# Fused pooled attention and Fourier-mixing feed-forward on one core: blocks mixed into attention in longer stretches, full price for a change of kind, one product per mean

## Chip, cores and metric

One Trainium2 chip, one core. The metric is the device time of one launch in microseconds, the median of several runs of the same program.

## What is computed

```python
q_pool = q.reshape(B, H, S // 2, 2, D).mean(axis=3)        # B 4, H 8, S 1152, D 64
attn = softmax(scale * q_pool @ k.T)                       # 576 x 1152 per head
x = (attn @ v), heads side by side                         # (4, 576, 512)
mixed = real(fft(fft(x, axis=1), axis=2))
u = x + mixed
un = (u - mean(u)) / sqrt(var(u) + 1e-6)                   # over the 512 features
out = u + relu(un @ w_ch1) @ w_ch2                         # 512 -> 2048 -> 512
```

Everything is float32. Products that need the accuracy are done as three products of high and low parts.

## The kernel before

The kernel is written by a planner that runs while the program is built: class `Model` keeps a clock for each engine, and `loop` chooses, piece by piece, what TensorE does next. The instructions then stand in that order in the program, on every engine.

**Attention.** 16 head pairs (four per batch), each with five units of 128 query columns. A unit on TensorE is three kinds of work. `S` (`s_piece`): score products of keys and queries, three pieces of 384 keys, high and low parts (`ksh`, `ksl`, `qh`, `ql`); VectorE scales each piece out of PSUM and takes the row extreme. `T` (`t_step`): transposes of the exponentials `sp` (ScalarE makes them in `s_exp`); VectorE or ScalarE copies them to `pt` and `ptc`. `AV` (`av`): products of `vs` and `pt` into the one bank `o`. The scores and transposes use 64 rows of the array, AV uses 64 columns, all else the full array.

**The middle of a batch** (`mid`, that is `dft` then `norm`): when four pairs are done, the two Fourier transforms are products with constant matrices (tiles `cc`, `cs`, `xs`, `bs`, `y`), then the mean over features (`lsum` with the matrix `onesm` of 1/512: two products per half of the columns, accumulated), the subtraction, the squares (`sq` with `onesm`), one over the root (`vt`, `dg`), and the high and low parts `unh`, `unl`. Its steps for VectorE, ScalarE and GpSimd are generators that `poll` drains whenever the engine would be free.

**The feed-forward** (`ffn`): per batch 32 blocks of 12 products, alternating four blocks with `w1` on `unh`, `unl` and four with `w2` on `g`. Batches 0 to 2 have blocks of 512 tokens; the last batch takes its own 576 and the 64 left over from each of the others in 64 blocks of 384 tokens. From the moment batch 0's middle is through, blocks are mixed into attention as filler: `spend` adds TensorE time to a `credit`, `block` takes it off, and the loop lets a block in while the credit is above 0 and its operands are ready (`fit`), or when nothing else is ready for `WAIT` of planner time. Behind the last pair `background` runs what is left; when no block fits it calls `force`, which takes the next step of the first waiting list, the middle of the batch ahead of the others.

**What sets the order.** For each candidate the loop adds, to the planner's time at which it is ready, `TURN` and half the entry of `SWITCH` if the kind of work changes:

```python
c = {k: max(t, now) + BIAS[k] + (0 if nc.mode == MODE[k] else TURN + 0.5 * SWITCH.get((nc.mode, MODE[k]), 130)) ...}
if fills and not lag[0]:
    if credit > 0 and fit():
```

**The start.** `load_first` brings the first pair in parts: keys in three parts, queries in the column ranges `Q0`; a part is pooled (two columns added), rounded to `qh` on ScalarE and subtracted to `ql`, on VectorE for the first part and on GpSimd for the others. Unit 0 needs columns 0 to 128, unit 1 columns 128 to 256.

Line 191 is the planner's call into the real instruction, so all rows have that line; rows are told apart by the tiles.

Of the kernel before, what the change touches and what calls it, by code (L numbers as in the profile page):

```python
# [195 lines left out]
class Pool:  # L196
# [4 lines left out]
    def tile(self, shape, dt, tag=None, name=None, bufs=None, **kw):  # L201
# [8 lines left out]
        if len(ring) == (bufs or self.bufs):  # L210
# [7 lines left out]
SWITCH = {("S", "T"): 95, ("T", "S"): 10, ("T", "AV"): 160, ("F", "S"): 222, ("T", "F"): 216, ("F", "AV"): 224, ("S", "AV"): 225,  # L218
          ("S", "F"): 285, ("S", "T1"): 95, ("T1", "S"): 10}
# [95 lines left out]
def fused_kernel(ctx: ExitStack, tc: tile.TileContext, k2, q2, v2, w1, w2, cst, out):  # L315
# [89 lines left out]
    Q0 = [(0, 128), (128, 512), (512, QW)]  # L405
# [112 lines left out]
    def den_recip(pr):  # L518
# [24 lines left out]
        if pr % 4 == 3:  # L543
            mids.append(Stream(mid(pr // 4), FIRST))
            started.append(pr // 4)

    def attention():
        idle = gp.tile([P, 512], F32, tag="g", name="zero")
        nc.vector.memset(idle, 0.0)
        ps = bank()  # L550
        for n in (512, 512, 192):
            nc.tensor.matmul(ps[:, :n], lhsT=idle[:, :P], rhs=idle[:, :n], start=True, stop=True)
        q_load, q_part, k_load, k_part, v_load = load_first()
        k_load(*K0[0])
        q_load(*Q0[0])
        for c in K0[1:]:
            k_load(*c)
        nc.sync.dma_start(ident, cst[4, :, :P])
        q_load(*Q0[1])
        v_load()  # L560
        q_load(*Q0[2])
        units = [(pr, j) for pr in range(NP) for j in range(5)]
        k_part(*K0[0])
        q_part(*Q0[0])
        k_part(*K0[1])
        k_part(*K0[2])
        for pc in range(3):
            s_piece(0, 0, pc)
        q_part(*Q0[1])
        s_exp(0, 0)  # L570
        s_exp(1, 0)
        nc.sync.dma_start(onesm, cst[4, :, P:2 * P])
        q_part(*Q0[2])
        loop(units)

    def loop(units):
# [136 lines left out]
        while at["a"][0] < n:  # L713
# [8 lines left out]
            c = {k: max(t, now) + BIAS[k] + (0 if nc.mode == MODE[k] else TURN + 0.5 * SWITCH.get((nc.mode, MODE[k]), 130)) for k, t in c.items() if t is not None}  # L722
            if fills and not lag[0]:
                if credit > 0 and fit():
# [14 lines left out]
    TURN = 100  # L739
    EXPS = 50  # L740
# [107 lines left out]
    def norm(b):  # L848
# [8 lines left out]
        for t in range(2):  # L857
            c = slice(t * HT, t * HT + HT)
            got = []

            def mean():
                got.append(bank())
                for j in range(2):
                    nc.tensor.matmul(got[0][:, :HT], lhsT=onesm, rhs=sm[:, j, c], start=j == 0, stop=j == 1)

            yield "pe", [sm[:, 0, c], sm[:, 1, c]], mean
# [257 lines left out]
    class Stream:  # L1124

        def __init__(self, gen, limit=None):
            self.gen, self.step, self.since, self.limit = gen, None, 0.0, limit or LIMIT
# [13 lines left out]
    def advance(s, pe=False, force=False):  # L1141
# [10 lines left out]
        if c[0] == "pe":  # L1152
            if not force and (not pe or nc.ready(*c[1]) > now + 50 or nc.slot("ps_t", "t", 7, 1) > now + 100):
                return False
# [46 lines left out]
    def spend(pe, at=False):  # L1201
        nonlocal credit
        credit = min(credit + pe * RATES[nb], 4000.0)
# [28 lines left out]
    WAIT, FLOOR = 500, -6000  # L1232

    def force():
        for s in list(mids)[:1] + streams:
            c = advance(s, True, True)
            if c:
                return True
            if c is None:
                if s in mids:  # L1240
                    mids.remove(s)
                else:
                    streams.remove(s)
                return True
        return False

    def background():

        while mids or fills or (tail[0] and streams):
            poll(True)  # L1250
            if fills and credit > 0 and fit():
                block()
                continue
            if not tail[0]:
                return
            if fills and fit():
                block()
            elif not force():
                if not (fills and block()):
                    return  # L1260
# [81 lines left out]
```

## Time and profile before

| | |
|---|---|
| median of 3 runs | 924.02 us (923.2 to 924.3) |
| profiled execution, its own time | 923.16 us |
| its span, first to last instruction | 921.4 us |
| TensorE busy | 895.4 us (97%) |
| VectorE busy | 592.0 us (64%) |
| ScalarE busy | 457.0 us (50%) |
| GpSimd busy | 289.6 us (31%) |
| mean granted TensorE clock | 0.996 |
| chain that ended last | TensorE 78%, VectorE 9%, ScalarE 5% |

TensorE's busy time includes ends that are modelled, so a wait of a few hundred nanoseconds between two products of the pipeline hides in it; for such waits the starts of successive rows are compared. The program has four stretches: attention alone (to about 235 us), attention with feed-forward blocks in between (to about 664 us), the middle of the last batch among blocks of batch 2 (to about 732 us), and feed-forward alone. A pair of rows with the same tiles is one instruction's two halves only for products of plain float32 (the mean, the squares, AV); a product of rounded float32 has one record.

### The profile page before, as it was taken

The numbers are of one execution on the slowest core, as the hardware profiler recorded it, in microseconds if no ns is written. First come the engines' busy times: TensorE is split into PE (matmuls) and PEld (weight loads), VectorE is DVE, ScalarE is ACT, GpSimd is POOL, SyncE is SP. The second block draws the span as 40 slices with busy tenths as digits, with TensorE's granted clock in tenths as the row PEclk, the third lists the DMA queues.
The fourth block names the chain that finished last, engine by engine and source line by source line (L and its number), as shares of the span: only waits on it lengthen the run. The fifth ranks groups of instructions, "written<-read, shape, count | busy, mean of one in ns | idle before, by whom it ended". The sixth has DMA issues, their size and how long they took to land.

```text
span 921.4 us, 22672 instructions
## 1 busy us (share of the span) xinstructions
PE 895.4 (97%) x9046; PEld 754.9 (82%) x9046; DVE 592.0 (64%) x1621; ACT 457.0 (50%) x916; POOL 289.6 (31%) x379
## 2 busy tenths in 40 slices
PE   8999998999999999999999999999999999999998
PEld 6888887787877788778777778887877788999998
DVE  6898889888769787779578655455474523222222
ACT  5678887769576468666444363545420311110110
POOL 4335456585438464555231330300030000000000
PEclk9999999999999999999999999999999999999999
DMA  6453664154675665777752242523284456543432
GB/s 217 132 177 106 217 207 133 61 189 156 215 263 219 202 238 205 259 237 282 250 197 70 104 136 91 186 70 105 80 249 134 129 189 211 192 135 117 135 92 69
DMA packets 54413, 153.27 MB, mean 166 GB/s; under 512 B 15186, under 2 KB 18018, under 8 KB 54308
## 3 DMA queue, kind: packets, MB, share of 16 engines
q1 hardware_dynamic: 49972, 142.20, 46.9%
q0 software_dynamic: 2160, 8.85, 2.9%
q8 instruction: 71, 1.16, 0.5%
q10 hardware_dynamic: 2176, 0.79, 0.3%
q14 instruction: 34, 0.28, 0.1%
HBM read 129.06 MB, written 22.75 MB: 165 GB/s over the span
## 4 chain that ended last, share of the span: by engine, by line
PE 78%; DVE 9%; ACT 5%; issue 4%; POOL 2%; DMA 1%; SPq 0%; DVEq 0%; ACTq 0%; POOLq 0%
PE f L191 46%; PE o L191 13%; PE s L191 12%; PE t L191 7%; DVE sp L191 3%; DVE pt L191 2%; ACT sp L191 2%; ACT pt L191 1%; POOL xs L191 1%; DVE wa L191 1%; DVE x L191 1%; DVE xs L191 1%; DMA qr<-in_q 1%; DVE d L191 0%; POOL wa L191 0%
## 5 line engine op out<-in xcount | busy, mean ns | idle before, releaser
L191 PE MATMUL f<-g,w 128*128 128x512 f32 (+1 forms) x960 | 211.6, 375 | 0.2 <-DVE sp L191 0.2
L191 ACT ACTIVATE sp<-sp,bia 128x1152 f32<-128x1152 f32 x144 | 180.2, 1257 | 38.4 <-DVE sp L191 37.9
L191 PEld LDWEIGHTS f<-g,w 128*128 128x128 f32 x960 | 173.7, 189 | 26.7 <-issue 2.8
L191 PE MATMUL f<-unh,w 128*128 128x512 f32 (+1 forms) x640 | 188.5, 376 | 0.0
L191 DVE TENSOR_SCALAR_CACHE_REDUCE sp<-s,bia 128x384 f32<-128x384 f32 x288 | 162.9, 612 | 15.5 <-PE s L191 12.3
L191 ACT ACTIVATE g<-f 128x512 fp32r<-128x512 f32 (+1 forms) x80 | 44.4, 555 | 234.5 <-PE f L191 234.5
L191 PE MATMUL o<-pt,vs 128*64 128x128 f32 (+1 forms) x2560 | 149.1, 266 | 2.4 <-ACT x L191 1.7
L191 PEld LDWEIGHTS o<-pt,vs 128*64 128x64 f32 x2560 | 127.1, 137 | 25.6 <-issue 19.1
L191 PEld LDWEIGHTS f<-unh,w 128*128 128x128 f32 x640 | 116.0, 188 | 18.5 <-issue 2.9
L191 DVE COPY pt<-t 128x512 f32<-128x512 f32 x143 | 92.3, 683 | 54.0 <-PE t L191 53.7
L191 PE MATMUL s<-ksh,qh 64*128 64x384 f32 (+1 forms) x432 | 111.2, 394 | 9.7 <-DVE pt L191 3.2
L191 PE MATMUL f<-unl,w 128*128 128x512 f32 (+1 forms) x320 | 118.0, 369 | 0.0
L191 DVE TENSOR_TENSOR x<-f,x 128x512 f32<-128x512 f32 (+1 forms) x80 | 47.7, 597 | 107.2 <-PE f L191 107.1
L191 DVE SCALAR_TENSOR_TENSOR g<-f,g 128x512 fp32r<-128x512 f32 (+1 forms) x80 | 50.8, 635 | 100.4 <-ACT g L191 100.3
L191 PEld LDWEIGHTS t<-ident,sp 64*128 64x128 f32 x2592 | 93.1, 139 | 24.9 <-issue 15.7
L191 PE MATMUL t<-ident,sp 64*128 64x64 f32 x2592 | 106.2, 226 | 2.9 <-DVE sp L191 1.3
L191 ACT COPY pt<-t 128x512 f32<-128x512 f32 x145 | 79.0, 590 | 36.9 <-PE t L191 36.0
L191 PE MATMUL s<-ksh,ql 64*128 64x384 f32 (+1 forms) x432 | 95.2, 348 | 0.6 <-POOL ql L191 0.6
L191 PE MATMUL s<-ksl,qh 64*128 64x384 f32 (+1 forms) x432 | 91.3, 338 | 0.0
L191 DVE TENSOR_SCALAR_CACHE_REDUCE sp<-s 128x384 f32<-128x384 f32 x144 | 74.7, 551 | 17.3 <-PE s L191 16.3
L191 POOL TENSOR_TENSOR wa<-wa,wk 128x256 int32<-128x256 int32 x64 | 47.3, 759 | 114.2 <-DVE wa L191 79.5
L191 PEld LDWEIGHTS s<-ksh,qh 64*128 64x128 f32 (+1 forms) x432 | 55.6, 188 | 33.6 <-DVE pt L191 8.2
(97 smaller groups left out, 1024.4 us busy)
## 6 DMA issues: line engine op xcount, KB each, us to landing
w<-w SPq DMA_DIRECT2D x128, 512.0 KB, 3.7
wraw<-in_w SPq DMA_DIRECT2D x32, 512.0 KB, 4.3
w<-wraw SPq DMA_DIRECT2D x32, 512.0 KB, 3.3
qr<-in_q SPq DMA_DIRECT2D x15, 640.0 KB, 4.8
vs<-in_v SPq DMA_DIRECT2D x16, 576.0 KB, 3.8
ksh<-in_k POOLq DMA_DIRECT2D x15, 576.0 KB, 6.0
kr<-in_k SPq DMA_DIRECT2D x15, 576.0 KB, 7.1
out<-x SPq DMA_DIRECT2D x12, 256.0 KB, 3.7
```

What stands on the lines that cost most here:

```text
L191: return real(*args, **kw)
```

## The change

- **Full price.** A change of kind is charged with the whole entry of `SWITCH` instead of half; the entries for transposes to scores go from 10 to 70 and for transposes to AV from 160 to 150.
- **Stretches by credit.** A block is let in by credit only above a threshold that depends on what TensorE is doing: 0 behind AV, 1000 behind scores or transposes, and down to -2000 behind another block. The credit may grow to 8000 instead of 4000, and `WAIT` goes from 500 to 300.
- **One product per mean.** The two halves of `lsum` are added by VectorE or GpSimd first, and the mean is one product instead of two, twice per batch.
- **Smaller first query loads.** The second query part is columns 128 to 256 instead of 128 to 512, the rest follows in two parts, and the load of the second part is issued ahead of the constant `ident`.
- **The end by readiness.** `background` lets a block in whenever one fits, and otherwise `force` takes whatever is ready first by the planner's clock: the next block, the middle of the batch or another list, instead of the first list in a fixed order.
- A parameter `SOFT` is added with the value 0, which changes nothing.

```diff
--- before.py
+++ after.py
@@ -215,8 +215,8 @@
         return t
 
 
-SWITCH = {("S", "T"): 95, ("T", "S"): 10, ("T", "AV"): 160, ("F", "S"): 222, ("T", "F"): 216, ("F", "AV"): 224, ("S", "AV"): 225,
-          ("S", "F"): 285, ("S", "T1"): 95, ("T1", "S"): 10}
+SWITCH = {("S", "T"): 95, ("T", "S"): 70, ("T", "AV"): 150, ("F", "S"): 222, ("T", "F"): 216, ("F", "AV"): 224, ("S", "AV"): 225,
+          ("S", "F"): 285, ("S", "T1"): 95, ("T1", "S"): 70}
 
 
 def _pe(m, op, out, ins, kw):
@@ -402,7 +402,7 @@
             mybir.DependencyClass.Sync, mybir.DependencyReason.DATA), reason="later than the first heads")
 
     K0 = [(i * 384, i * 384 + 384) for i in range(3)]
-    Q0 = [(0, 128), (128, 512), (512, QW)]
+    Q0 = [(0, 128), (128, 256), (256, 512), (512, QW)]
 
     def load_first():
 
@@ -541,7 +541,7 @@
         for c in (slice(0, HT), slice(HT, SQ)):
             yield ("pool", "dve") if pr % 4 < 3 else ("dve", "pool"), lambda e: ENG[e].tensor_tensor(x[:, c], x[:, c], big[:, c], op=ALU.mult)
         if pr % 4 == 3:
-            mids.append(Stream(mid(pr // 4), FIRST))
+            mids.append(Stream(mid(pr // 4), FIRST, SOFT if 0 < pr // 4 < B - 1 else 0))
             started.append(pr // 4)
 
     def attention():
@@ -555,10 +555,11 @@
         q_load(*Q0[0])
         for c in K0[1:]:
             k_load(*c)
+        q_load(*Q0[1])
         nc.sync.dma_start(ident, cst[4, :, :P])
-        q_load(*Q0[1])
         v_load()
         q_load(*Q0[2])
+        q_load(*Q0[3])
         units = [(pr, j) for pr in range(NP) for j in range(5)]
         k_part(*K0[0])
         q_part(*Q0[0])
@@ -571,6 +572,7 @@
         s_exp(1, 0)
         nc.sync.dma_start(onesm, cst[4, :, P:2 * P])
         q_part(*Q0[2])
+        q_part(*Q0[3])
         loop(units)
 
     def loop(units):
@@ -719,9 +721,9 @@
             exp()
             now = nc.t["pe"]
             c = {k: f() for k, f in (("s", s_cand), ("t", t_cand), ("a", a_cand))}
-            c = {k: max(t, now) + BIAS[k] + (0 if nc.mode == MODE[k] else TURN + 0.5 * SWITCH.get((nc.mode, MODE[k]), 130)) for k, t in c.items() if t is not None}
+            c = {k: max(t, now) + BIAS[k] + (0 if nc.mode == MODE[k] else TURN + SWITCH.get((nc.mode, MODE[k]), 130)) for k, t in c.items() if t is not None}
             if fills and not lag[0]:
-                if credit > 0 and fit():
+                if credit > THR.get(nc.mode, 0) and fit():
                     block()
                     continue
                 if (not c or min(c.values()) > now + WAIT) and credit > FLOOR and fit():
@@ -737,6 +739,8 @@
     BIAS = {"s": 0.0, "t": 0.0, "a": 0.0}
     MODE = {"s": "S", "t": "T", "a": "AV"}
     TURN = 100
+    THR = {"AV": 0, "S": 1000, "T": 1000, "F": -2000, "M": 0}
+    SOFT = 0
     EXPS = 50
 
     def room(pr, j):
@@ -856,14 +860,16 @@
         vt = smp.tile([HT // 3, 6], F32, tag="vt", name="vt")
         for t in range(2):
             c = slice(t * HT, t * HT + HT)
+            yield SB, lambda e: ENG[e].tensor_tensor(sm[:, 0, c], sm[:, 0, c], sm[:, 1, c], op=ALU.add)
+        for t in range(2):
+            c = slice(t * HT, t * HT + HT)
             got = []
 
             def mean():
                 got.append(bank())
-                for j in range(2):
-                    nc.tensor.matmul(got[0][:, :HT], lhsT=onesm, rhs=sm[:, j, c], start=j == 0, stop=j == 1)
-
-            yield "pe", [sm[:, 0, c], sm[:, 1, c]], mean
+                nc.tensor.matmul(got[0][:, :HT], lhsT=onesm, rhs=sm[:, 0, c], start=True, stop=True)
+
+            yield "pe", [sm[:, 0, c]], mean
             ps = got[0]
             d = mtile([P, 4, HT], F32, "d")
             for i, u in enumerate((ua, ub)):
@@ -1123,8 +1129,8 @@
 
     class Stream:
 
-        def __init__(self, gen, limit=None):
-            self.gen, self.step, self.since, self.limit = gen, None, 0.0, limit or LIMIT
+        def __init__(self, gen, limit=None, soft=0):
+            self.gen, self.step, self.since, self.limit, self.soft = gen, None, 0.0, limit or LIMIT, soft
 
         def peek(self):
             if self.step is None:
@@ -1150,7 +1156,7 @@
             return False
         now = nc.t["pe"]
         if c[0] == "pe":
-            if not force and (not pe or nc.ready(*c[1]) > now + 50 or nc.slot("ps_t", "t", 7, 1) > now + 100):
+            if not force and (not pe or nc.mode in MODE.values() and now - s.since < s.soft or nc.ready(*c[1]) > now + 50 or nc.slot("ps_t", "t", 7, 1) > now + 100):
                 return False
             c[2]()
         else:
@@ -1200,7 +1206,7 @@
 
     def spend(pe, at=False):
         nonlocal credit
-        credit = min(credit + pe * RATES[nb], 4000.0)
+        credit = min(credit + pe * RATES[nb], 8000.0)
         poll(at)
 
     def step(queue):
@@ -1229,35 +1235,42 @@
             step(fills)
         return need[0] is not None and nc.ready(*need[0]) <= nc.t["pe"] + 100 and nc.slot("ps_t", "t", 7, 1) <= nc.t["pe"] + 100
 
-    WAIT, FLOOR = 500, -6000
+    WAIT, FLOOR = 300, -6000
+
+    def when(s):
+
+        c = s.peek()
+        if c is False:
+            return 0.0, s
+        if c is None:
+            s.step = None
+            return 1e12, s
+        if c[0] == "pe":
+            return max(nc.ready(*c[1]), nc.slot("ps_t", "t", 7, 1)), s
+        return min(nc.probe(c[1], e) for e in c[0] if e != "now"), s
 
     def force():
-        for s in list(mids)[:1] + streams:
-            c = advance(s, True, True)
-            if c:
-                return True
-            if c is None:
-                if s in mids:
-                    mids.remove(s)
-                else:
-                    streams.remove(s)
-                return True
-        return False
+        best = min((when(s) for s in list(mids)[:1] + streams), key=lambda x: x[0], default=(1e12, None))
+        if need[0] is None and fills:
+            step(fills)
+        if need[0] is not None and max(nc.ready(*need[0]), nc.slot("ps_t", "t", 7, 1)) <= best[0]:
+            return block()
+        s = best[1]
+        if best[0] >= 1e12:
+            return bool(fills) and block()
+        if advance(s, True, True) is None:
+            if s in mids:
+                mids.remove(s)
+            else:
+                streams.remove(s)
+        return True
 
     def background():
 
-        while mids or fills or (tail[0] and streams):
+        while mids or fills or streams:
             poll(True)
-            if fills and credit > 0 and fit():
-                block()
-                continue
-            if not tail[0]:
+            if not (fills and fit() and block()) and not force():
                 return
-            if fills and fit():
-                block()
-            elif not force():
-                if not (fills and block()):
-                    return
 
     def conversions():
         nonlocal cdue
```


Three places in the two programs' orders show how instructions move. In them `o` is AV, `t` a transpose, `s` a score product, `f<-g` or `f<-unh`, `f<-unl` a feed-forward block, `f<-lsum`, `f<-onesm,sq` and `f<-dg` the middle of a batch.

TensorE near the end of attention (pair 15), before: one block stands inside a unit's AV products.

```order
L191 MATMUL s<-ksl,qh 128x384 x2
L191 MATMUL o<-pt,vs 64x128 x6
L191 MATMUL f<-g,w_9092 128x512 x12
L191 MATMUL o<-pt,vs 64x128 x10
L191 MATMUL o<-ptc,vs 64x128 x2
L191 MATMUL t<-ident,sp 128x64 x36
```

The same unit of the changed program:

```order
L191 MATMUL s<-ksl,qh 128x384 x2
L191 MATMUL f<-g,w_9784 128x512 x12
L191 MATMUL f<-g,w_9918 128x512 x12
L191 MATMUL o<-pt,vs 64x128 x16
L191 MATMUL o<-ptc,vs 64x128 x2
L191 MATMUL t<-ident,sp 128x64 x36
```

Two blocks now stand ahead of AV, and the AV products of a unit are not parted. Over the whole of attention 60 blocks in 59 separate places become 58 blocks in 43 places, and the number of times that the kind of work changes on TensorE (scores, transposes, AV, blocks, the middle, the transposes of `den`) goes from 435 to 414; counted by the part of the array that is in use (64 rows, 64 columns, all) it goes from 296 to 287.

TensorE in the last batch's middle, from the second mean to the spread of one over the root, before:

```order
L191 MATMUL f<-lsum,onesm 128x288 x2
L191 MATMUL f<-unh,w_10943 128x512 x2
L191 MATMUL f<-unl,w_10943 128x512
...
L191 MATMUL f<-unl,w_10943 128x512
L191 MATMUL f<-onesm,sq 96x1 x6
L191 MATMUL f<-g,w_10963 128x512 x12
L191 MATMUL f<-dg,onesm 128x288
L191 MATMUL f<-g,w_10987 128x512 x12
L191 MATMUL f<-dg,onesm 128x288
```

Changed:

```order
L191 MATMUL f<-lsum,onesm 128x288
L191 MATMUL f<-unh,w_10947 128x512 x2
L191 MATMUL f<-unl,w_10947 128x512
...
L191 MATMUL f<-unl,w_10947 128x512
L191 MATMUL f<-g,w_10967 128x512 x12
L191 MATMUL f<-g,w_10991 128x512 x12
L191 MATMUL f<-onesm,sq 96x1 x6
L191 MATMUL f<-g,w_11016 128x512 x12
L191 MATMUL f<-g,w_11047 128x512 x12
L191 MATMUL f<-dg,onesm 128x288
```

The mean is one product, three blocks instead of one stand between the second mean and the squares, and two blocks instead of one stand behind them. Ahead of this, nine blocks instead of seven stand between the last AV product and the first Fourier product (`f<-cs,xs`).

GpSimd at the start, before:

```order
L191 TENSOR_TENSOR ksl<-kr,ksh 128x192 x4
L191 TENSOR_TENSOR qr<-qr 128x384
L191 TENSOR_TENSOR ql<-qr,qh 128x384
L191 TENSOR_TENSOR qr<-qr 128x128
L191 TENSOR_TENSOR ql<-qr,qh 128x128
L191 DMA ksh<-in_k 128x1152
```

Changed:

```order
L191 TENSOR_TENSOR ksl<-kr,ksh 128x192 x4
L191 TENSOR_TENSOR qr<-qr 128x128
L191 TENSOR_TENSOR ql<-qr,qh 128x128
L191 TENSOR_TENSOR qr<-qr 128x256
L191 TENSOR_TENSOR ql<-qr,qh 128x256
L191 TENSOR_TENSOR qr<-qr 128x128
L191 TENSOR_TENSOR ql<-qr,qh 128x128
```

GpSimd does the 128 columns that unit 1 needs first, then 256 columns instead of having them in the same instruction. On SyncE the load of these 128 columns stands ahead of `ident` instead of behind it, and the load of the other 256 columns behind the load of `vs`. ScalarE rounds the 256 columns behind the first two exponentials, where it rounded the last 128 before.

## Rows read from the trace of the kernel before

**Rows 1.** The page, busy time and share of the span by engine.
```profile
PE 895.4 (97%) x9046; PEld 754.9 (82%) x9046; DVE 592.0 (64%) x1621; ACT 457.0 (50%) x916; POOL 289.6 (31%) x379
```

**Rows 2.** Busy us (x instructions) by stretch: PE, PEld, DVE, ACT, POOL; then PEclk, DMA.
```profile
43.00:235.00 192.00, 183.42 (x2822) 156.93 (x2818) 166.54 (x520) 156.57 (x314) 109.72 (x143) 1.00 0.47 155
120.00:165.00 45.00, 41.15 (x673) 35.04 (x669) 41.94 (x129) 37.67 (x73) 30.98 (x41) 1.00 0.45 147
235.00:664.00 429.00, 423.31 (x4444) 339.19 (x4442) 294.78 (x784) 237.36 (x485) 152.06 (x197) 1.00 0.53 180
728.00:732.00 4.00, 4.00 (x12) 3.07 (x12) 0.89 (x3) 2.22 (x8) 0.00 (x0) 0.61 0.34 86
```

**Rows 3.** TensorE waits, 43 to 235 us: total, times, longest; first and last of 10.
```profile
PE s L191 <- DVE pt L191: 2.4, 5, 1.2
...
PE t L191 <- ACT sp L191: 0.2, 1, 0.2
```

**Rows 4.** The same from 235 to 664 us; first and last of 10.
```profile
PE f L191 <- ACT y L191: 1.3, 1, 1.3
...
PE s L191 <- DVE sp L191: 0.2, 1, 0.2
```

**Rows 5.** Order of time at the start: start, length, engine, line, operation, [idle <-releaser].
```profile
8.69 0.99 POOL L191 TENSOR_TENSOR qr<-qr 128x384 f32<-128x384 f32 x1 [0.78 <-DMA qr<-in_q]
...
10.28 0.44 PE L191 MATMUL s<-ksh,qh 64*128 64x384 f32 x2 [1.87 <-ACT qh L191]
...
11.36 0.69 PE L191 MATMUL s<-ksh,ql 64*128 64x384 f32 x2 [0.64 <-POOL ql L191]
...
11.38 1.24 ACT L191 ACTIVATE sp<-sp,bia 128x1152 f32<-128x1152 f32 x1
...
14.08 1.38 PE L191 MATMUL t<-ident,sp 64*128 64x64 f32 x36
```

**Rows 6.** Order of time on TensorE, the mean products of batch 0.
```profile
192.33 2.21 PE L191 MATMUL f<-lsum,onesm 128*128 128x288 f32 x8
...
194.47 0.44 PE L191 MATMUL s<-ksh,qh 64*128 64x384 f32 x2
```

**Rows 7.** Order of time on TensorE, where the kind of work changes.
```profile
657.15 1.97 PE L191 MATMUL o<-pt,vs 128*64 128x128 f32 x32
658.94 0.39 PE L191 MATMUL o<-ptc,vs 128*64 128x128 f32 x4
659.26 0.77 PE L191 MATMUL t<-ident,sp 64*128 64x64 f32 x18
659.97 0.73 PE L191 MATMUL f<-unh,w 128*128 128x512 f32 x2
...
662.82 0.27 PE L191 MATMUL t<-ident,den 128*9 128x128 f32 x1
```

**Rows 8.** Order of time on TensorE, feed-forward blocks one behind the other.
```profile
740.28 0.62 PE L191 MATMUL f<-unh,w 128*128 128x512 f32 x2
...
743.00 0.62 PE L191 MATMUL f<-unh,w 128*128 128x512 f32 x2
```

**Rows 9.** Order of time on TensorE, from transposes to score products.
```profile
95.09 0.42 PE L191 MATMUL s<-ksh,qh 64*128 64x384 f32 x2
95.35 0.34 PE L191 MATMUL s<-ksh,ql 64*128 64x384 f32 x2
95.53 0.33 PE L191 MATMUL s<-ksl,qh 64*128 64x384 f32 x2
```

**Rows 10.** Order of time on TensorE, the last batch behind attention.
```profile
685.83 0.43 PE L191 MATMUL f<-cs,xs 128*97 128x128 f32 x2 [1.28 <-DVE xs L191]
...
724.10 0.67 PE L191 MATMUL f<-onesm,sq 128*96 128x1 f32 x6 [0.70 <-POOL sq L191]
...
726.18 0.64 PE L191 MATMUL f<-onesm,sq 128*96 128x1 f32 x6 [1.42 <-DVE sq L191]
726.68 4.58 PE L191 MATMUL f<-g,w 128*128 128x512 f32 x12
731.08 0.67 PE L191 MATMUL f<-dg,onesm 96*128 96x288 f32 x2
```


## The prediction

> **What bounds the kernel.** I read the share of busy time by engine first: TensorE 97% of the span, VectorE 64%, ScalarE 50% [rows 1]. That alone says that work taken off TensorE counts nearly in full, but also that the page's idle time (26 us) is an upper bound on what better hiding can show there. The stretches come second [rows 2]. From 43 to 235 us, attention with nothing to fill in, TensorE is idle for 192.0 - 183.4 = 8.6 us and VectorE is busy for 166.5 of 192 us, 87%; from 120 to 165 us it is 41.9 of 45, 93%, and there TensorE is idle for 3.85 us. From 235 to 664 us, with blocks to fill in, TensorE is idle for 5.7 us of 429. So TensorE is the bound, with VectorE close behind in the first stretch only. The list of waits is third: in both stretches they are many and short, at most 1.2 to 1.3 us for one, down to 0.2 [rows 3, 4]. Last, in order of time, the two ends, where whole gaps stand [rows 5, 10], and the places where the kind of work changes [rows 7 to 9].
>
> **The change, part by part.**
>
> *One product per mean.* Eight products of batch 0's and its like's means go (two per batch, four batches). In batch 0 four of them, eight records, take 192.33 to 194.47 = 2.14 us up to the next score product [rows 6]. Of that some 0.15 us is the change of kind, so a record is 0.25 us and a product 0.5; eight are **-3.9 us**. With nothing taken off it would be 4.3, and if half were covered 2.0. Eight additions of 288 columns come in, on VectorE or GpSimd; TensorE stands among blocks or score products there, so I cost them at nothing. In the last batch, where the chain is bare, they are counted under the end.
>
> *Fewer changes of kind.* 435 become 414, 21 fewer. What one costs: four AV records take 658.94 to 659.26 = 0.32 us, where the 32 ahead of them take 1.79, 0.056 each; so leaving AV costs 0.32 - 0.22 = 0.10. A block behind transposes takes 659.97 to 662.82 = 2.85 us [rows 7], one behind another block 740.28 to 743.00 = 2.72 [rows 8]; so entering a block costs 0.13. A change is thus 0.1 if one side pays, 0.23 if both do; I take 0.15, since most changes that go are those around a block, which pay on both sides, but leave a cheaper one behind. 21 x 0.15 = **-3.2 us**, between -2.1 and -4.8. The credit thresholds do this: the blocks move from 59 places to 43.
>
> From transposes to scores, both on 64 rows of the array, the first score pair takes 95.09 to 95.35 = 0.26 us and the next 0.18 [rows 9], so 0.08 is paid without any change of the array's division; the new entry of 70 in the table is near that, the old 10 was not. The Trainium skill (TensorEngine Tiling (Array Packing), Key Properties) says that a change of the tiling mode drains TensorE, and that using another tile of the same mode does not. By that rule alone only the 296 to 287 mode changes would count, 9 x 0.15 = 1.4 us, and the whole sum would be 1.8 us smaller. The trace agrees as to the modes, but shows a price inside one as well, so I keep 3.2.
>
> *The end.* Three gaps of the last batch's middle stand open [rows 10]: 1.28 us ahead of the first Fourier product, which waits for VectorE's `xs`; 0.70 and 1.42 us ahead of the two groups of squares. Behind them TensorE runs the next block, 12 products, from 726.68 to 731.08 = 4.40 us instead of 2.72: the clock granted from 728 to 732 us is 0.61 of full speed on average [rows 2], and it fell behind the gaps. That is 1.28 + 2.12 + 1.68 = 5.1 us. The new order has two blocks more ahead of the Fourier product (5.4 us against 1.3 missing) and two more ahead of the squares (5.4 against 2.1). The extra addition before the mean (0.44 to 0.86 us by the neighbours' lengths on VectorE and GpSimd) fits in that cover as well. I take **-5.0 us**; the ends are 0 (the blocks then wait for their weights instead) and -5.1. With no gap there, nothing should lower the clock.
>
> *The start.* The products of unit 1 wait 1.87 us for `qh` and 0.64 us for `ql` [rows 5]: GpSimd gets the 384 columns at 8.69 us and needs 0.99 us for the first of two like steps. With 128 columns first, loaded earlier, GpSimd can begin when it is free (0.78 us before 8.69), the first step is about a third as long, and the scores of unit 1 can begin near 8.7 instead of 10.28. What is late next is the second exponential, which ends at 11.38 + 1.24 and does not move, because it hangs on VectorE's work on unit 0; the transposes, at 14.08 now, can then start for the first head at once and be done some 2 us sooner. The other 256 columns are rounded behind the exponentials and may hold unit 2 for a few tenths. **-1.8 us**, between 0 and -2.5 (both waits). SyncE issues one more load; `ident`, which moves behind it, is needed only for those transposes, more than 8 us later.
>
> *The rest of attention.* Every unit is reordered, so the short waits fall elsewhere. Nothing in the trace prices the new ones. The bounds: all visible idle from 43 to 664 us goes, -14.3, or there is as much again, +14.3. I take **0**, since the same work meets the same engines and the mean wait is a few tenths of a microsecond.
>
> Sum: -3.9 - 3.2 - 5.0 - 1.8 = -13.9 us. The profiled execution took 923.16 us (span 921.4, 1.8 around it), so 909.3; the median of the runs is 0.9 above that execution, so **910.0 us**.
>
> **Rivals.**
>
> *Waits left open (slower).* Filling in fewer places takes the cover away from 16 spots where a block stood. If each then shows a wait as long as the longest of today, 1.2 us [rows 3], that is +19.2 against -13.9: 929. It turns from gain to loss at 13.9 / 16 = 0.87 us a spot. For it: the thresholds of 1000 behind scores and transposes keep blocks out exactly where the waits for VectorE and ScalarE are. Against: most waits are 0.2 to 0.5 us, and a wait over `WAIT`, now 300, still lets a block in.
>
> *VectorE takes over.* In the first stretch it has 7 to 13% left [rows 2]. The first blocks come later (none by the end of the eighth pair, where there were five), so that stretch grows by about 14 us of TensorE work without cover. If the rate of 120 to 165 us, 3.85 us idle in 45, held for 45 us more, that is +3.9, and the start's 1.8 would be given back: 915.7. The Trainium skill (the same page, PSUM Bottleneck) warns of this: packing small products speeds TensorE up, but not the copies out of PSUM, which can become the bound. The trace bears it out for one stretch of 45 us, not for the whole.
>
> *The end waits for weights.* If the blocks moved forward there find their weights late, the 5.0 us turn into another wait: 915.0. For it: seven blocks in a row each need a tile of weights. Against: blocks in a row run at 2.72 us from 740 us on [rows 8].
>
> *Waits shrink too.* If the truer prices halve the visible idle between 43 and 664 us (14.3), it is 7 us better: 903.
>
> *The change does nothing* is excluded by the order of the programs.
>
> **How the numbers follow.** The forecast, with some microseconds either way for the reordered waits: 0.45. VectorE: 0.20. Weights late: 0.10. Waits shrink: 0.13. Several of the losses together, ending near 924: 0.05. Waits left open: 0.07. A measurement of this kernel can tell 0.2%, 1.85 us, from no change. So faster 0.88, no difference 0.05, slower 0.07. The range holds the first four cases with their spread, 903 to 919 us, and leaves out the last two and the edges of the others, about 2 in 10.
>
> **What would show it.** Right: 16 records of the mean instead of 32; no wait of a microsecond ahead of `f<-cs,xs` and the squares of the last batch, and the granted clock at 1.00 throughout that part; the scores of unit 1 near 8.7 us; the last block's start some 13 us earlier. The prediction is wrong if TensorE's idle time from 43 to 664 us is up by several microseconds, if the waits for VectorE grow above all in the first stretch, or if blocks in the last part wait for loads.

## The result and the profile after

| | before | after |
|---|---|---|
| median, four runs each in turn | 923.61 us (922.11 to 924.3) | 907.73 us (906.37 to 909.87) |
| profiled execution, its own time | 923.16 us | 906.37 us |
| its span | 921.4 us | 904.6 us |

The ratio is 0.9832, with an interval from 0.9809 to 0.9856: 15.9 us faster by the medians, 16.8 between the two profiled executions. The forecast was 910.0.

The page's busy time of the changed kernel, against [rows 1]: TensorE is up to 98% of the span, with 16 records fewer.

```profile
PE 883.0 (98%) x9030; PEld 752.2 (83%) x9030; DVE 606.8 (67%) x1646; ACT 451.6 (50%) x902; POOL 291.4 (32%) x379
```

The same stretches of the changed kernel as in [rows 2] (length, then busy us of PE, PEld, DVE, ACT, POOL; granted clock, DMA):

```profile
43.00:235.00 192.00, 185.56 (x2864) 159.39 (x2860) 171.15 (x532) 151.71 (x300) 100.96 (x129) 1.00 0.42 143
120.00:165.00 45.00, 44.25 (x698) 38.18 (x700) 42.05 (x131) 38.55 (x77) 21.76 (x27) 1.00 0.38 128
235.00:664.00 429.00, 423.23 (x4417) 345.96 (x4416) 311.42 (x812) 236.97 (x479) 167.05 (x216) 1.00 0.57 193
```

In the first stretch (43 to 235 us) TensorE now sits idle for 6.4 us instead of 8.6. Between 120 and 165 us it is 0.75 instead of 3.85, while VectorE is as full as before (42.05 of 45). From 235 to 664 us it is 5.8 after 5.7.

TensorE's waits in the changed kernel from 235 to 664 us, for [rows 4] (total, times, longest), are headed by a new one, for the weights of one block in batch 1's part:

```profile
PE f L191 <- DMA w<-w: 2.5, 1, 2.5
PE s L191 <- DVE pt L191: 0.9, 4, 0.4
PE f L191 <- ACT y L191: 0.7, 1, 0.7
```

The start of the changed kernel in order of time, for [rows 5]:

```profile
8.77 0.44 PE L191 MATMUL s<-ksh,qh 64*128 64x384 f32 x2 [0.30 <-ACT qh L191]
...
9.83 1.26 ACT L191 ACTIVATE sp<-sp,bia 128x1152 f32<-128x1152 f32 x1 [1.12 <-DVE sp L191]
...
11.23 0.71 PE L191 MATMUL t<-ident,sp 64*128 64x64 f32 x16 [0.28 <-ACT sp L191]
```

Unit 1's scores begin at 8.77 instead of 10.28 us, and the transposes at 11.23 instead of 14.08, as soon as the first exponential is there.

The last batch's middle of the changed kernel in order of time, for [rows 10]. Ahead of it stands the second product with `dg`, which ends batch 2's middle; the row with 24 products of `g` is two blocks:

```profile
657.32 0.65 PE L191 MATMUL f<-dg,onesm 96*128 96x288 f32 x2
...
674.08 0.46 PE L191 MATMUL f<-cs,xs 128*97 128x128 f32 x2 [2.49 <-DVE xs L191]
...
704.02 0.65 PE L191 MATMUL f<-lsum,onesm 128*128 128x288 f32 x2
...
715.97 1.10 PE L191 MATMUL f<-onesm,sq 128*96 128x1 f32 x12
716.93 5.74 PE L191 MATMUL f<-g,w 128*128 128x512 f32 x24
722.51 0.65 PE L191 MATMUL f<-dg,onesm 96*128 96x288 f32 x2
```

The squares wait for nothing, and the two blocks behind them take 5.58 us from start to start at full clock (716.93 to 722.51), where one took 4.40 at the lower. But the wait ahead of the first Fourier product has not gone: it has grown from 1.28 to 2.49 us.

**Where the 16.8 us came from.** In both kernels 67 blocks stand ahead of the last batch's first Fourier product. It starts 11.75 us earlier (674.08 instead of 685.83), and what is left behind it is 5.05 us shorter (230.52 instead of 235.57 us to the end of the span). For a finer split I gave each kind of work on TensorE one price, from the starts of rows before, and subtracted these prices from the starts in both traces; what is left is waiting. Without waits, TensorE's program went from 856.7 to 849.6 us (-7.1). The waits went from 55.4 to 45.7 (-9.7): -2.0 in the first pair, -4.7 in the fifteen others, -2.8 behind attention. This split is my own working with fitted prices, an estimate that no view shows; it agrees with the two differences above.

### The profile page after: what moved, and what is told of

It is laid out like the page before. It is cut to its first block, busy times and chain, and to the rows that moved or that the text cites. A ratio compares the mean times of both kernels' runs of the same rounds, so it can differ in the third digit from the quotient of the medians.

```text
span 904.6 us, 22635 instructions
## 1 busy us (share of the span) xinstructions
PE 883.0 (98%) x9030; PEld 752.2 (83%) x9030; DVE 606.8 (67%) x1646; ACT 451.6 (50%) x902; POOL 291.4 (32%) x379
## 4 chain that ended last, share of the span: by engine, by line
PE 81%; DVE 9%; issue 4%; ACT 3%; DMA 1%; POOL 1%; DVEq 0%; ACTq 0%; POOLq 0%
PE f L191 48%; PE o L191 13%; PE s L191 13%; PE t L191 8%; DVE sp L191 3%; DVE pt L191 2%; DVE xs L191 1%; DMA w<-w 1%; ACT sp L191 1%; DVE wa L191 1%; DVE d L191 1%; DVE x L191 1%; ACT x L191 0%; DVE tmp L191 0%; DVE g L191 0%
## 5 line engine op out<-in xcount | busy, mean ns | idle before, releaser
L191 PE MATMUL f<-g,w 128*128 128x512 f32 (+1 forms) x960 | 207.4, 372 | 0.0
L191 DVE COPY pt<-t 128x512 f32<-128x512 f32 x158 | 101.0, 683 | 35.3 <-PE t L191 35.2
L191 PE MATMUL s<-ksh,qh 64*128 64x384 f32 (+1 forms) x432 | 115.2, 389 | 4.6 <-DVE pt L191 1.2
L191 PE MATMUL s<-ksh,ql 64*128 64x384 f32 (+1 forms) x432 | 99.0, 345 | 0.1
L191 PE MATMUL s<-ksl,qh 64*128 64x384 f32 (+1 forms) x432 | 94.9, 336 | 0.0
L191 ACT COPY pt<-t 128x512 f32<-128x512 f32 x130 | 70.5, 589 | 28.6 <-PE t L191 28.2
L191 PEld LDWEIGHTS s<-ksh,qh 64*128 64x128 f32 (+1 forms) x432 | 59.7, 186 | 26.1 <-DVE pt L191 6.3
```

What stands on the lines that cost most here:

```text
L191: return real(*args, **kw)
```

## Experiments

Each run was timed in turn with the kernel before on the same chip. "Against before" is the difference of the two medians there; kernels of different chips are compared by it alone. The changed kernel itself stands at -15.9, and in a second series (`e5_after_again`) at -12.9 us. So one and the same kernel moves by 3 us between series, and a difference of that size between kernels of different series decides nothing. The experiments stand by question, not in the order in which they ran.

### What is the new order of the end worth?

`e3_end` is the kernel before with the new `force` and `background` alone; `e4_old_end` is the changed kernel with the old ones.

```diff
 e3_end: kernel before
+    def when(s): ...
-        for s in list(mids)[:1] + streams:
+        best = min((when(s) for s in list(mids)[:1] + streams), ...)
 e4_old_end: changed kernel, the same lines the other way
```

> The kernel before with the end by readiness alone; attention is the same instruction for instruction. Separate-terms theory: three blocks instead of one ahead of the squares close the two waits of 0.70 and 1.42 us and give back 1.7 us of half clock, while the wait of 1.28 us ahead of the Fourier product stays: about -3.8 us, 919.7. Rival, the waits only move to the weights' loads: within 1 us of 923.5.

Measured: 918.96 us, -3.3, ratio 0.9964 (0.9951 to 0.9976). The trace of `e3_end` has the wait ahead of the Fourier product as it was, none ahead of the squares, and blocks at full speed behind them:

```profile
684.99 0.43 PE L191 MATMUL f<-cs,xs 128*97 128x128 f32 x2 [1.28 <-DVE xs L191]
...
727.83 1.10 PE L191 MATMUL f<-onesm,sq 128*96 128x1 f32 x12
728.79 5.74 PE L191 MATMUL f<-g,w 128*128 128x512 f32 x24
```

So the part of the term on the squares, 2.12 of waiting and 1.68 of lower clock, 3.8 us, was right; the 1.28 was not in this edit.

> The changed kernel with the old end. Separate-terms theory: the end costs what its own waits showed, 3 to 5 us more than the changed kernel's 907.7, so 911 to 913. Rival, the parts depend on each other: as the chain of the last batch lies bare here too, 920 to 925.

Measured: 932.36 us, +10.1, ratio 1.0099 (1.0076 to 1.0123). Both theories were far too small. In the order of time on TensorE:

```profile
657.96 1.13 PE L191 MATMUL f<-dg,onesm 96*128 96x288 f32 x4
676.14 0.74 PE L191 MATMUL f<-cs,xs 128*97 128x128 f32 x2 [17.05 <-DVE xs L191]
...
678.67 1.61 PE L191 MATMUL f<-g,w 128*128 128x512 f32 x4
...
715.89 1.33 PE L191 MATMUL f<-dg,onesm 96*128 96x288 f32 x2 [2.99 <-ACT dg L191]
```

and in its windows of 10 us (columns as above) TensorE stands still for the whole of the first:

```profile
660.00:670.00 10.00, 0.00 (x0) 0.00 (x0) 9.62 (x23) 2.67 (x4) 0.00 (x0) 0.63 0.34 96
670.00:680.00 10.00, 3.86 (x16) 3.65 (x17) 7.85 (x22) 1.01 (x3) 0.00 (x0) 0.52 0.00 0
```

No block stands between `dg` and the Fourier product. By the code, the next block in line is one on `g`, which needs the block just issued; the old `force`, finding it not ready, takes the next step of the middle whenever that may be ready. The whole chain that leads to `xs` lies bare: 17.05 us, then products at half the clock. The new `force` asks which of the two is ready first and takes the block. In the kernel before, six blocks stand at that place. So the end's new order is worth 3.3 us in the kernel before and by the medians 23 to 26 us in the changed one (10.1 against -12.9 and -15.9). Not all of that is the end's: in the profiled execution of `e4_old_end` attention ends 6.6 us later than in that of the changed kernel, in the same order, and its granted clock is 0.56 from 180 to 190 us and 0.83 from 210 to 220, where the other has 1.00. Of the 28.3 us between the two spans (932.9 and 904.6) about 22 are left for the end.

### Do the other parts work alone, with the old end?

`e1_product` is the kernel before with one product per mean, `e2_plan` with the full price and the credit thresholds.

```diff
 e1_product: kernel before
+            yield SB, lambda e: ENG[e].tensor_tensor(sm[:, 0, c], sm[:, 0, c], sm[:, 1, c], op=ALU.add)
-                for j in range(2):
-                    nc.tensor.matmul(got[0][:, :HT], lhsT=onesm, rhs=sm[:, j, c], start=j == 0, stop=j == 1)
+                nc.tensor.matmul(got[0][:, :HT], lhsT=onesm, rhs=sm[:, 0, c], start=True, stop=True)
 e2_plan: kernel before
-SWITCH ... TURN + 0.5 * SWITCH ... credit > 0 ... 4000.0 ... WAIT = 500
+SWITCH ... TURN + SWITCH ... credit > THR ... 8000.0 ... WAIT = 300
```

> The kernel before with the one-product means alone. Separate-terms theory: 3.9 us of TensorE work goes and the kinds of work change about as often (431 against 433 times, the mean and the other full-array products counted as one kind), so about 919.5 against 923.5, -0.42%. Rival, new order decides: the planner moves 57 instead of 60 blocks into attention and all short waits fall elsewhere, so anything within 5 us of 923.5, and not near -3.9.

> The kernel before with the full price and the stretches, but two products per mean, the old first loads and the old end. Separate-terms theory: fewer changes of kind (395 against 433) give about -5 us in attention, whatever the end does, so about 918.5. Rival, the parts depend on each other: in this program no block at all stands between the end of batch 2's middle and the first Fourier product of batch 3, where six stood, so that chain of some 17 us lies bare, with half the clock behind it, and the kernel is slower than before, 930 to 936.

Measured: 942.65 us, +20.4, ratio 1.0219 (1.0193 to 1.0245), and 934.78 us, +12.5, ratio 1.0142 (1.0124 to 1.0159). The first was expected faster and came out as the slowest kernel of the study. Taking eight products away cannot cost 20 us by itself; what it did was to move every later choice of the planner. The first line of TensorE's list of waits in `e1_product` is

```profile
PE f L191 <- DVE xs L191: 16.4, 1, 16.4
```

and in `e2_plan`

```profile
PE f L191 <- DVE xs L191: 17.9, 2, 17.1
```

the same bare chain as in `e4_old_end`. The second run came out as its rival said, 930 to 936. With the new end the same two edits stand at -0.7 and -6.3 us (`e9_product` and `e10_plan` below), so the old end costs them 21.1 and 18.8 us: the loss is the end's.

### And with the new end?

Four pieces, each on top of `e3_end`: `e8_start` (smaller query loads), `e9_product`, `e10_plan` (price and thresholds), and the two halves of the last, `e11_price` and `e12_stretch`.

```diff
 each: kernel before + the new end
+e8_start:    Q0 = [(0, 128), (128, 256), (256, 512), (512, QW)], its loads and parts
+e9_product:  the lines of e1_product
+e10_plan:    the lines of e2_plan
+e11_price:   SWITCH, TURN + SWITCH
+e12_stretch: credit > THR, 8000.0, WAIT = 300
```

> The kernel before with the end by readiness and the new first loads. Theory: 2.0 us less in the first pair than with the end alone, 918.96 in the run above, but five blocks instead of six ahead of the Fourier product cost 1.2 us there, and the changes of kind are 427 instead of 433, so 918. Rival, the reordering of attention decides: anywhere from 914 to 924.

> The kernel before with the end by readiness and one product per mean. Theory: against the end alone (918.96) 3.9 us less for the products, 1.2 us more ahead of the Fourier product (five blocks instead of six): 916.3. Rival, the product merge was what made the run with it alone slow: over 925.

> The kernel before with the end by readiness, the full price and the stretches. Theory: with the end safe, fewer changes of kind give 5 us against the end alone by the counted switches (405 against 433), less 1.2 us ahead of the Fourier product: 915. Rival, the short waits grow with the longer stretches: 919 or more.

> The kernel before with the end by readiness and the full price alone. Theory: the price alone hardly changes the places of blocks (55 for 57 blocks, 436 changes of kind), so within 2 us of the end alone, 917 to 921.

> The kernel before with the end by readiness and the credit thresholds alone. Theory: 62 blocks in 53 places and 432 changes, so within 2 us of the end alone as well, 917 to 921; only price and thresholds together take the changes down to 405. Rival, the thresholds bring the gain by themselves: 915 or less.

| | median us | against before | ratio (interval) | against `e3_end` |
|---|---|---|---|---|
| `e8_start` | 938.31 | +15.4 | 1.0158 (1.0135 to 1.018) | +18.7 |
| `e9_product` | 922.98 | -0.7 | 0.9996 (0.9973 to 1.002) | +2.6 |
| `e10_plan` | 917.33 | -6.3 | 0.9926 (0.991 to 0.9942) | -3.0 |
| `e11_price` | 928.40 | +4.8 | 1.0053 (1.0032 to 1.0075) | +8.1 |
| `e12_stretch` | 914.96 | -8.7 | 0.9905 (0.989 to 0.992) | -5.4 |

On top of the end, start, product and plan come to +18.7 + 2.6 - 3.0 = +18.3 us; made together they bring 9.6 to 12.6 us on top of it. The parts do not add, since each one moves the whole order behind it. Of the expectations only the rival for `e12_stretch` came true (915 or less); `e8_start` lies outside even its rival's range, `e11_price` outside its own, and `e9_product` and `e10_plan` between theory and rival. The 2.6 us of `e9_product` and the 3.0 of `e10_plan` are no more than the spread between series, and the executions of `e9_product` go from 917.31 to 928.79 us.

In each of the three that lost, windows of 10 us inside attention show a lower clock (the column behind the five engines). In `e8_start` it is behind four waits of 0.2 to 0.7 us, in `e11_price` among batch 1's Fourier products, of which a group waits 2.45 us for `y`:

```profile
470.00:480.00 10.00, 10.00 (x71) 8.70 (x71) 8.98 (x24) 9.29 (x16) 8.48 (x11) 0.70 0.39 118
```

```profile
280.00:290.00 10.00, 7.55 (x61) 5.84 (x60) 5.99 (x13) 4.92 (x12) 3.10 (x5) 0.83 0.46 150
```

In `e9_product` the clock is 0.83 from 340 to 350 us, where a score product waits:

```profile
341.49 0.45 PE L191 MATMUL s<-ksh,qh 64*128 64x384 f32 x2 [3.14 <-ACT pt L191]
```

That these falls carry all of each loss was not isolated, and they do not tell the losers from the rest: `e10_plan`, which gained, has 0.83 from 460 to 470 us, behind waits of 0.55, 0.70, 0.20 and 0.27 us. For `e8_start`, whose profiled execution is its fastest and 5.4 us below its median, most of the 18.7 stays open; its own part did what it should, with the last AV products of the first pair starting at 41.13 instead of 43.48 us (42.33 in `e3_end`).

The end differs as well. `e8_start`, `e9_product`, `e10_plan` and `e11_price` wait 2.5 us for `xs`, with a granted clock of 0.83 to 0.90 in a window of 10 us behind it; `e3_end` waits 1.28 and keeps its clock, and `e12_stretch` does not wait there. So the four carry 1.2 us and more that is not their own edit's.

The last two rows also bear on the plan's own account. By one count of kind changes over the orders (433 before, 413 after), `e12_stretch` has 432, `e11_price` 436, and only the two together 405: by kinds, the thresholds alone remove none. Counted by the part of the array in use it is otherwise. The score products of each pair's fifth unit use the whole array (128*128 in their rows), as blocks do; the count of 296 and 287 took them for 64 rows. By the forms in the traces there are 323 such changes before, 301 in the changed kernel, 326 in `e11_price`, 302 in `e12_stretch` and 287 in `e10_plan`. So the thresholds alone remove 21, nearly as many as the whole change (22). In `e12_stretch` 15 blocks start behind such scores, in the kernel before 2:

```profile
648.50 0.34 PE L191 MATMUL s<-ksl,qh 128*128 128x384 f32 x1
648.68 0.62 PE L191 MATMUL f<-unh,w 128*128 128x512 f32 x2
649.14 0.39 PE L191 MATMUL f<-unl,w 128*128 128x512 f32 x1
...
689.31 0.38 PE L191 MATMUL f<-cs,xs 128*97 128x128 f32 x2
```

The block's first pair takes 0.46 us here from start to start, as it does inside a row of blocks; behind transposes it takes 0.56 [rows 7, 659.97 to 660.53]. By the prediction's 0.15 us a change, 21 are 3.2 us, and the missing wait for `xs` is 1.3: together 4.5 of the 5.4, an estimate that no run isolates.

### Why is the Fourier product still late?

`e5_after_again` is the changed kernel, unedited. `e7_late` lets the last batch's first Fourier product in 2.7 us later, so that one more block stands ahead of it.

```diff
 e7_late: changed kernel, in advance
-... nc.ready(*c[1]) > now + 50 or ...
+... nc.ready(*c[1]) > now + (-2700 if tail[0] and fills and <an operand is bs> else 50) or ...
```

> The changed kernel once more, on the chip on which the next three run, so that they can be set against it: 907.7 us, with executions 2 to 3 us apart where the granted clock falls in one and not in the other.

> The changed kernel with the first Fourier product of the last batch let in 2.7 us of planner time later, so that one more block stands ahead of it (six instead of five). Theory: that chain begins when batch 2's middle ends, not with the last AV product, and lacks 2.49 us of cover, so the wait goes and the kernel gains 2 to 2.5 us on the changed kernel, 905.5; a few tenths may come back ahead of the squares, which have two blocks instead of three. Rival, VectorE finishes xs later as it serves the added block first: no gain.

Measured on the same chip: `e5_after_again` 910.01 us, -12.9, ratio 0.9851 (0.9832 to 0.987); `e7_late` 903.97 us, -18.9, ratio 0.9807 (0.9788 to 0.9826). The two rows of `e7_late`, by window and in order of time:

```profile
675.00:695.00 20.00, 20.00 (x105) 16.64 (x104) 10.38 (x23) 4.29 (x11) 0.00 (x0) 1.00 0.55 175
```

```profile
678.20 0.43 PE L191 MATMUL f<-cs,xs 128*97 128x128 f32 x2
```

and of `e5_after_again`:

```profile
675.00:695.00 20.00, 17.52 (x82) 14.54 (x81) 11.27 (x26) 3.88 (x10) 0.00 (x0) 0.91 0.46 147
```

```profile
679.70 0.66 PE L191 MATMUL f<-cs,xs 128*97 128x128 f32 x2 [2.48 <-DVE xs L191]
```

One more block of 2.7 us takes the 2.48 us wait away, and with it the lower clock behind it: 0.09 of 20 us, some 1.8. That is 4.3 of the 6.0 us between the medians. The wait is in all three traces with this order there (2.48 to 2.49 us, `e6_twice` being the third); the 1.8 need not be, for the changed kernel's first profiled execution kept 1.00 behind it. The fastest executions lie 4.1 us apart (907.54 and 903.42). The waits for weights in batch 1's part differ too: in `e5_after_again`

```profile
PE f L191 <- DMA w<-w: 2.4, 2, 1.8
```

and in `e7_late`

```profile
PE f L191 <- DMA w<-w: 0.7, 2, 0.5
```

The edit does not touch those blocks, and the same block waits 2.45 us in the changed kernel's first trace and 1.15 in that of `e6_twice`, so I take these 1.7 us for chance; that is not shown. `e7_late` beats both kernels and has the lowest median of the study.

### What is one product of the mean worth?

`e6_twice` issues each of the changed kernel's eight mean products twice, with every other instruction in its old place; the second overwrites the first, so the output is unchanged.

```diff
 e6_twice: changed kernel
+                nc.nc.tensor.matmul(got[0][:, :HT], lhsT=onesm, rhs=sm[:, 0, c], start=True, stop=True)
                 nc.tensor.matmul(got[0][:, :HT], lhsT=onesm, rhs=sm[:, 0, c], start=True, stop=True)
```

> The changed kernel with each of the eight mean products issued twice, the second over the first; the planner does not see the added one, so all else stands in the same order. Theory: the price of eight products alone is 3.9 us, 911.6. Rival, they are partly covered by waits next to them: less than 2 us more.

Measured: 912.25 us (906.97 to 914.48), ratio 0.9879 (0.9856 to 0.9901), 2.2 us above `e5_after_again`, whose interval overlaps: by the times, inconclusive. The order of time in its trace is sharper (L870 is the added call):

```profile
518.84 0.65 PE L870 MATMUL f<-lsum,onesm 128*128 128x288 f32 x2
519.32 0.65 PE L191 MATMUL f<-lsum,onesm 128*128 128x288 f32 x2
519.81 0.65 PE L870 MATMUL f<-lsum,onesm 128*128 128x288 f32 x2
520.29 0.65 PE L191 MATMUL f<-lsum,onesm 128*128 128x288 f32 x2
```

From start to start a product takes 0.48 to 0.49 us here; over all eight places the added ones take 4.0 us (0.48 to 0.59 each).

## Why the prediction was right, and where not

The whole came out 2.3 us below the forecast by the medians, inside its range. (909.3 and 0.9 make 910.2 and not 910.0, and the longest wait of [rows 3]'s list is 1.3 and not 1.2; neither changes the argument.) Point by point:

**One product per mean, -3.9: right.** There are 16 records instead of 32, nothing on TensorE waits for the added sums, and `e6_twice` shows 4.0 us for eight products in place. But that is the term inside a fixed order. As an edit of its own it brought no gain with the new end (-0.7 us, interval 0.9973 to 1.002) and cost 20.4 with the old.

**Fewer changes of kind, -3.2: agrees, not isolated.** TensorE's program without waits fell by 7.1 us, the 3.9 and 3.2 of the sum; the prices are the ones fitted before, so this tests the count and not the price. The rival sum of 1.4 us rests on the count of 296 to 287; by the forms of the trace it is 323 to 301, 22 changes fewer where the kinds are 21 fewer, so the two rules give the same sum here and this change cannot tell them apart. "The credit thresholds do this" holds by the part of the array (302 with the thresholds alone) and not by kinds (432).

**The end, -5.0: here a step failed.** The squares' 3.8 us went as said. The failed step is "two blocks more ahead of the Fourier product (5.4 us against 1.3 missing)". I counted the blocks from the last AV product. But the last batch's middle is polled only when batch 2's has ended, so its chain starts at the second product with `dg`, and only the blocks behind that cover it. The kernel before has that product here:

```profile
667.57 0.65 PE L191 MATMUL f<-dg,onesm 96*128 96x288 f32 x2
```

From there to its Fourier product [rows 10] lie 18.3 us with six blocks; in the changed kernel it is 674.08 - 657.32 = 16.8 us with five, and the wait is 1.2 us longer. One block less is 2.7 us of cover, but the chain itself is 1.5 us shorter: GpSimd made part of `xs` before, VectorE makes all of it now (why it is shorter was not isolated). `e7_late`, with the shorter chain and six blocks, has no wait. So the sign "no wait of a microsecond ahead of `f<-cs,xs`" failed, and -5.0 should have been -3.8 + 1.2 = -2.6, and by my split of the waits it was -2.8.

I also gave the end a floor of 0 as if the old order were harmless beside the other parts. `e4_old_end` shows that it was the part on which the whole hangs.

**The start, -1.8: right.** The scores of unit 1 begin at 8.77 us (forecast 8.7), and by my split the waits up to the end of the first pair are 2.0 us less. The size is good to some half a microsecond: the wait for `qh` is 1.1 to 2.2 us in the eight traces with the old loads and at most 0.5 in those with the new.

**The rest of attention, 0: it was -4.7,** inside the bounds of 14.3 either way; of the visible idle time from 43 to 664 us 2.1 us went (14.3 to 12.2). The -4.7 is a remainder: it hangs on the -3.2 for the changes of kind, and no run isolates it. The end's shortfall of 2.2 to 2.4 us took back half of it, so the sum looks better than its terms; that is luck.

**The rivals.** VectorE did not take over: between 120 and 165 us TensorE's idle time fell to 0.75 us with VectorE at the same 93%, so an engine that full was not the limit there; the waits were a matter of order. Waits left open: idle 5.8 after 5.7 us from 235 to 664, with 43 places instead of 59; the total did not grow. Weights at the end: no wait for them from 664 us on; the one of 2.5 us stands in batch 1's part. Waits shrink too: in part, as above.

The price of a single part cannot be read off as I wrote the sum, term on term. The terms hold for the two orders that were compared; they do not hold for the edits one at a time.

## What to carry to other kernels

Where a planner writes the order, judge an edit on the whole new order, and first look at what covers the longest bare chain: a chain of 17 us, hidden before by a row of six blocks, lay bare behind two small edits and cost them 19 and 21 us. Count cover only from the moment at which the chain's first step is released, not from the last visible landmark ahead of it, and take the chain's length from the new order. A wait of one to three microseconds on TensorE is to be priced with the work behind it, which can run at half the clock.

## What the runs showed of the hardware

The same program, in the same order and with the same wait, kept its clock in one execution and lost it in another. The changed kernel's profiled execution, in order of time in batch 0's middle:

```profile
178.99 0.71 PE L191 MATMUL t<-ident,sp 64*128 64x64 f32 x15 [1.80 <-ACT y L191]
...
180.65 1.73 PE L191 MATMUL f<-cs,y 97*128 97x289 f32 x6
```

and `e5_after_again`, the same instructions:

```profile
179.65 0.71 PE L191 MATMUL t<-ident,sp 64*128 64x64 f32 x15 [1.80 <-ACT y L191]
...
181.29 3.11 PE L191 MATMUL f<-cs,y 97*128 97x289 f32 x6
```

Its granted clock from 182 to 184 us (column behind the engines) is 0.50, that is 1.2 GHz; in the other execution it stays at 1.00, 2.4 GHz:

```profile
182.00:184.00 2.00, 2.00 (x5) 1.14 (x4) 0.00 (x0) 1.29 (x3) 0.00 (x0) 0.50 0.00 0
```

Both waited 1.80 us for `y` before. Behind that, six products take 1.73 us in one and 3.11 in the other, and pair 7 ends 5.5 us later, of which 0.7 were there before. `e4_old_end` and `e7_late`, in the same order up to there, lost it too (0.56 and 0.54 from 180 to 190 us), and `e6_twice` kept it. So behind a wait of this length the clock can fall or stay, and executions of one kernel lie up to 6 us apart (907.54 to 913.62) without any change. The Trainium skill (TensorE: Matmul & The Clock Gate, Part 1: The HAM clock gate) says that the stretch over which the gate looks at TensorE's activity is not tied to the program's start, so that the same kernel can meet it differently. The two traces agree with that, and cannot show it to be the cause.
